# Layer 1 with tokens on the partitions: 512 moving columns, h turned by DMA, layer 2 four products later

## The chip, the cores and the metric

The kernel runs on one core of one Trainium2 chip. The metric is the device time in microseconds, the median of several runs. All of the work is in one launch; inputs and outputs are float32 in DRAM.

## The reference

Sliding-window attention with a linear bias is followed by a mixture of eight experts. After attention, x has 4608 tokens of 512 values. Cut to what matters:

```python
logits = x @ w_gate                      # 4608 x 8
P = np.exp(logits - logits.max())
for _ in range(8):                       # rows and columns in turn
    P /= P.sum(1, keepdims=True) + 1e-09
    P /= P.sum(0, keepdims=True) + 1e-09
    P *= N / E
out = np.zeros((N, D))
for e in range(8):
    h = np.maximum(x @ w1[e], 0.0)       # 512 -> 1024
    out += P[:, e:e + 1] * (h @ w2[e])   # 1024 -> 512
```

Every token goes through every expert; P only weights the results.

## The kernel before, in words

**Two stages.** To about 320 us the kernel computes attention, one batch after the other, and fills TensorE's gaps with both layers of experts 0 and 1 (`Filler`, `unit_atoms`, whose layer 2 is L159); their unweighted results go to DRAM (`ysp`), and x goes there too, by token (`xd`). Then P is balanced in eight rounds (`balance`). The second stage, from about 321 us to the end, does experts 2 to 7. It is the one that changes.

**The second stage** walks 108 units, a unit being 256 tokens and one expert: 18 groups of 256 tokens, experts 2 to 7 inside each. Matrices are cut in quarters, and each layer is done in Strassen's way with seven products instead of eight. Units 4 and 5 (experts 6 and 7 of the first group) do layer 1 plainly, since their weight sums are not yet made (`l1_bank`, L990), and the last unit does layer 2 plainly (`plain`, L1115).

**Layer 1 of a unit.** ScalarE scales the 256 tokens of x by that expert's P (`scale_x`, L923: P is not negative, so relu(P x w) is P relu(x w)), SP turns the result by two DMA transposes so that features are on the partitions (`turn_xs`, L935), and VectorE forms four sums (`sums_x`, L947). Seven parts follow (`part`, L1014), each of eight matmuls at L1020 with 128 weight columns stationary and 128 tokens moving. They add up in three PSUM banks A, B and C; between them ScalarE copies A to B (L1182), C to `s5` (L1186) and B to C (L1194), since sums are shared. h then leaves as four quarters (slots 0 to 3 of `hs`): slots 0 and 2 straight by relu, slots 3 and 1 by an add of `s5` on VectorE (L1203, L1209) and a relu in place (L1033). Features are on the partitions, which is what layer 2 needs of its stationary operand.

**Layer 2 of a unit.** `make_sums` (L1035) forms the sums of h's quarters on VectorE, and `product` (L1048) runs seven products of four matmuls with 256 moving columns (L1057). The products of the six experts of a group add up in four PSUM banks (`Ms`); at the group's end `gather` (L1082) adds them into `acc`, `begin` (L1069) brings in experts 0 and 1 from `ysp` (loaded by `load_y`), and `finish` (L1103) writes `acc` out.

**Order.** It is written out by hand in the loop at L1163. Each engine takes its instructions in the order of the program. TensorE alternates a part of unit n with a product of unit n-1. `scale_x` and `turn_xs` work two units ahead. `some` feeds VectorE sums of weights that later experts need, in the first eleven units. SP's queue carries the turns, the loads of x and y and the stores of the output; POOL's queue carries loads of weights, the last of them `load_w2` of expert 7 for the plain layer 2 of the last unit.

Of the kernel before, what the change touches and what calls it, by code (L numbers as in the profile page):

```python
# [14 lines left out]
def kernel(  # L15
# [20 lines left out]
    P = 128  # L36
# [68 lines left out]
    def unit_atoms(e, b0, nb, pool, tag, bufs, finish):  # L105
# [5 lines left out]
        halves = 2 if e == 0 and b0 < RI else 1  # L111
# [140 lines left out]
    if True:  # L252
# [649 lines left out]
        N = len(units)  # L902
        HF = Fd // 2
        h: dict = {}
        Ms: dict = {}
# [4 lines left out]
        xtok = [acc.rearrange("p m d -> p (m d)").bitcast(FP16)[:, HD * i : HD * i + HD] for i in range(2)]  # L910
        xs = [xset[i // 2][:, 4 + 2 * (i % 2) : 6 + 2 * (i % 2), :].rearrange("p q n -> p (q n)") for i in range(4)]

        def strassen(n):
            return n >= E - 2 or units[n][1] < E - 2

        def load_x(g):
            for m in range(2):
                nc.sync.dma_start(out=xtok[m], in_=xd[2 * g + m])

        load_x(groups[0])  # L920
        balance(7)

        def scale_x(n):  # L923
            if n >= N:
                return
            g, e = units[n]
            for m in range(2):
                blk = 2 * g + m
                nc.scalar.mul(out=xs[2 * (n % 2) + m], in_=xtok[m], mul=P_sb[:, blk, e : e + 1])  # L929
            if e == E - 1 and n + 1 < N:  # L930
                if g == groups[0]:
                    xtok[:] = [per.tile([P, HD], FP16, name=f"xtok_{i}", tag="yo", bufs=YO) for i in range(2)]
                load_x(units[n + 1][0])

        def turn_xs(n):  # L935
            if n >= N:
                return
            for m in range(2):
                nc.sync.dma_start(
                    out=xset[n % 2][:, 2 * m : 2 * m + 2, :].rearrange("p q (d t) -> p (q d) t", t=P),  # L940
                    in_=xs[2 * (n % 2) + m],
                    transpose=True,
                )
# [3 lines left out]
        def sums_x(n):  # L947
            if n >= N or not strassen(n):
                return
            x = xset[n % 2]  # L950
            nc.vector.tensor_tensor(out=x[:, T1 : T3 + 1], in0=x[:, B12 : B22 + 1], in1=x[:, B11 : B12 + 1 : 2], op=ALU.subtract)
            nc.vector.tensor_tensor(out=x[:, T2], in0=x[:, T3], in1=x[:, B11], op=ALU.add)
            nc.vector.tensor_tensor(out=x[:, T4], in0=x[:, B21], in1=x[:, T2], op=ALU.subtract)
# [33 lines left out]
        def new_h(n):  # L987
            h[n] = per.tile([P, 8, NF2, P], FP16, name=f"hs_{n}", tag="hT", bufs=2)

        def l1_bank(n, i):  # L990
            g, e = units[n]
            if i == 0:
                new_h(n)
            x = xset[n % 2][:, 0:4].rearrange("p q (d t) -> p (q d) t", t=P).rearrange("p (b d) t -> p d b t", b=2)
            ps = aps.tile([P, 2, HB], FP32, name=f"psh_{n}_{i}", tag="pmm", bufs=4)
            for f in range(2):
                ft = 2 * i + f
                for dt in range(NDT):
                    nc.tensor.matmul(  # L999
                        out=ps[:, f, :],  # L1000
                        lhsT=W1L[e][:, dt, P * ft : P * ft + P],
                        rhs=x[:, dt],
                        start=(f == 0 and dt == 0),
                        stop=(dt == NDT - 1),
                        skip_group_check=True,
                    )
            fh, j = 2 * (i // 2), 2 * (i % 2)
            nc.scalar.activation(
                out=h[n][:, fh : fh + 2, j : j + 2, :].rearrange("p t f k -> p f t k"),
                in_=ps.rearrange("p f (t k) -> p f t k", t=2),  # L1010
                func=AF.Relu,
            )

        def part(n, ps, w, x, start=False):  # L1014

            q = SL[units[n][1]][w]
            q = q if isinstance(q, list) else [q[:, k] for k in range(2)]
            for j in range(NF2):
                for k in range(2):
                    nc.tensor.matmul(  # L1020
                        out=ps[:, j, :],
                        lhsT=q[k][:, P * j : P * j + P],
                        rhs=xset[n % 2][:, x, P * k : P * k + P],
                        start=(start and j == 0 and k == 0),
                        stop=(k == 1),
                        skip_group_check=True,
                    )

        def bank(n, name):
            return aps.tile([P, NF2, P], FP32, name=f"ps{name}_{n}", tag="pmm", bufs=4)  # L1030

        def relu(n, slot, src):
            nc.scalar.activation(out=h[n][:, slot], in_=src, func=AF.Relu)  # L1033

        def make_sums(n):  # L1035
            t = h[n]
            nc.vector.tensor_tensor(out=t[:, 4:6], in0=t[:, 0:2], in1=t[:, 2:4], op=ALU.add)  # L1037
            nc.vector.tensor_tensor(out=t[:, 6:8], in0=t[:, 1:4:2], in1=t[:, 0:3:2], op=ALU.subtract)
            nc.vector.tensor_tensor(out=t[:, 1], in0=t[:, 0], in1=t[:, 3], op=ALU.add)

        LEFT = {3: 0, 4: 3, 5: 4, 2: 5, 6: 6, 7: 7, 1: 1}
        RIGHT = {1: "f1", 2: "q11", 3: "f3", 4: "f4", 5: "q22", 6: "f6", 7: "f7"}
        BANK = {3: (0, 0), 4: (0, 1), 5: (1, 0), 2: (1, 1), 6: (2, 0), 7: (2, 1), 1: (3, 0)}

        def ends(n):
            return n >= 0 and units[n][1] == (E - 2 if units[n][0] == groups[-1] else E - 1)

        def product(n, *which):  # L1048
            if n < 0:
                return  # L1050
            g, e = units[n]
            for m in which:
                bk, half = BANK[m]
                if bk not in Ms:
                    Ms[bk] = mps.tile([P, 2, 2 * P], FP32, name=f"psM_{bk}")
                for f in range(NF2):
                    nc.tensor.matmul(  # L1057
                        out=Ms[bk][:, half, :],
                        lhsT=h[n][:, LEFT[m], f, :],
                        rhs=W2L[e][RIGHT[m]][:, f, :],  # L1060
                        start=(e == 2 and f == 0 and half == 0),
                        stop=(ends(n) and f == NF2 - 1 and (half == 1 or m == 1)),
                        skip_group_check=True,
                    )

        def load_y(g, e):
            nc.sync.dma_start(out=y, in_=ysp[e, 2 * g : 2 * g + 2].rearrange("m p d -> p m d"))
# [14 lines left out]
        def gather(g, *which):  # L1082
            q4 = acc.rearrange("p m (c n) -> p (m c) n", c=2)
            for m in which:
                bk, half = BANK[m]
                ps = Ms[bk][:, half, :]
                for lo, step, op in {
# [53 lines left out]
        while filler.l1 or filler.todo or len(filler.l2) > 3:  # L1141
# [3 lines left out]
            if pieces == 2:  # L1145
                scale_x(1)
                turn_xs(1)
# [138 lines left out]
```

## Time and profile before

| | |
|---|---|
| median of three runs | 1003.1 us (1002.57 to 1004.06) |
| the profiled execution | 1001.61 us |
| its span, first to last instruction | 999.8 us |
| TensorE, VectorE, ScalarE busy in 360 to 960 us | 100%, about 79%, about 83% |
| DMA engines' mean busy share, 500 to 900 us | 0.35 to 0.41 |
| HBM read and written | 78.30 MB, 23.59 MB |

In the profile PE is TensorE's matmuls, PEld its weight loads, DVE VectorE, ACT ScalarE, POOL GpSimd and SP the engine that issues most DMAs. A row of groups gives line, engine and operation, output and inputs, shape and count, then busy time and the mean of one, then the idle time before it and who ended it. Matmuls are pipelined, so the duration of one (219 ns for 128 columns) says less than the distance between two starts. A timeline row gives start, length, engine, line and count. Of a DMA the profile gives the time its issue takes on the queue and the time to its landing.

### The profile page before, as it was taken

How to read it: one execution, taken by the hardware profiler on the slowest of the kernel's cores; microseconds unless marked ns; L12 is line 12 of the kernel's file. 1: busy time of each engine (PE TensorE's matmuls, PEld its weight loads, DVE VectorE, ACT ScalarE, POOL GpSimd, SP SyncE). 2: the span in 40 equal slices, each digit the busy share in tenths (PEclk: the TensorE clock that was granted, in tenths of full speed). 3: DMA queues.
4: the chain of work that ended last, by engine and by line, in shares of the span. 5: the costliest groups of instructions: out<-in, count | busy, mean ns of one | idle time of the engine just before them, and what ended most of it. 6: DMA issues, size and time to landing. Idle time of an engine off the chain costs nothing.

```text
span 999.8 us, 28277 instructions
## 1 busy us (share of the span) xinstructions
PE 988.3 (99%) x11731; PEld 816.0 (82%) x11731; DVE 762.0 (76%) x1593; ACT 718.0 (72%) x1216; POOL 110.0 (11%) x202
## 2 busy tenths in 40 slices
PE   7999999999999999999999999999999999999998
PEld 5645665566545899999999999999999999999997
DVE  5737677665688989887887787787787787787787
ACT  7655545554435768888888888888888888888885
POOL 3314444354110000000000000000000000000000
PEclk9999999999999999999999999999999999999999
DMA  9998999989997324333333433333433433333371
GB/s 250 212 271 218 187 233 230 234 170 183 222 201 152 81 54 97 82 61 94 86 56 95 86 76 75 88 73 75 96 76 65 99 78 65 96 76 66 96 116 49
DMA packets 264978, 123.08 MB, mean 123 GB/s; under 512 B 204433, under 2 KB 255633, under 8 KB 264849
## 3 DMA queue, kind: packets, MB, share of 16 engines
q1 hardware_dynamic: 249152, 100.65, 45.4%
q0 software_dynamic: 15264, 20.46, 11.5%
q8 instruction: 92, 1.51, 0.6%
q14 instruction: 38, 0.30, 0.1%
q10 hardware_dynamic: 432, 0.16, 0.1%
HBM read 78.30 MB, written 23.59 MB: 102 GB/s over the span
## 4 chain that ended last, share of the span: by engine, by line
PE 91%; DVE 5%; ACT 2%; DMA 1%; issue 1%; DVEq 0%; ACTq 0%
PE psM L1057 31%; PE psB L1020 14%; PE psy L159 11%; PE psA L1020 9%; PE psC L1020 9%; PE psh L137 9%; PE psh L118 3%; PE psS L457 1%; PE psN L491 1%; DVE pt L468 1%; DMA k<-in_k_dram 1%; ACT pt L463 1%; PE psh L999 1%; DMA xset<-xs 1%; DVE xsb L502 1%
## 5 line engine op out<-in xcount | busy, mean ns | idle before, releaser
L1057 PEld LDWEIGHTS <-hs 128*128 128x128 f16 x2996 | 271.0, 98 | 22.4 <-DVE hs L1037 0.4
L1057 PE MATMUL psM<-w2l,hs 128*128 128x256 f16 x1440 | 186.6, 273 | 0.2 <-DVE hs L1037 0.2
L1020 PEld LDWEIGHTS <-w1l 128*128 128x128 f16 x2848 | 181.4, 98 | 4.8 <-issue 0.4
L1033 ACT ACTIVATE hs<-hs 128x512 f16<-128x512 f16 x212 | 130.4, 629 | 36.2 <-DVE hs L1203 26.6
L1203 DVE TENSOR_TENSOR hs<-psB,s5y 128x512 f16<-128x512 f32 x106 | 73.3, 692 | 97.9 <-ACT xs L929 92.2
L1020 PEld LDWEIGHTS <-s 128*128 128x128 f16 x2136 | 141.6, 98 | 6.7 <-issue 0.2
L929 ACT ACTIVATE xs<-xtok,L_sb 128x512 f16<-128x512 f16 x204 | 135.8, 720 | 2.1 <-DMA xset<-xs 2.1
L159 PE MATMUL psy<-w2t,hT 128*128 128x512 f16 x576 | 135.3, 379 | 0.0
L1057 PE MATMUL psM<-more,hs 128*128 128x256 f16 x864 | 129.5, 273 | 0.0
L1020 PE MATMUL psB<-xset,s 128*128 128x128 f16 x1424 | 108.5, 219 | 0.1
L1020 PE MATMUL psA<-xset,w1l 128*128 128x128 f16 x1424 | 108.5, 219 | 0.0
L149 ACT ACTIVATE hT<-psh 128x512 f16<-128x512 f32 (+1 forms) x104 | 60.1, 581 | 63.5 <-PE psh L137 63.4
L159 PEld LDWEIGHTS <-hT 128*128 128x128 f16 x576 | 54.0, 98 | 58.2 <-issue 1.1
L463 ACT ACTIVATE pt<-psS 128x1024 f16<-128x1024 f32 x64 | 64.6, 1022 | 50.4 <-PE psS L457 49.9
L137 PE MATMUL psh<-xT,w1t 128*128 128x512 f16 (+1 forms) x448 | 99.0, 364 | 0.0
L1037 DVE TENSOR_TENSOR hs<-hs 128x1024 f16<-128x1024 f16 x107 | 73.9, 691 | 20.6 <-ACT hs L1033 18.6
L1194 ACT COPY psC<-psB 128x512 f32<-128x512 f32 x106 | 60.4, 570 | 38.6 <-PE psB L1020 38.6
L579 DVE CAST yo<-psy 128x512 f16<-128x512 f32 x65 | 44.6, 690 | 50.8 <-PE psy L159 50.1
L1186 ACT COPY s5y<-psC 128x512 f32<-128x512 f32 x106 | 62.2, 587 | 22.4 <-PE psC L1020 22.4
L615 POOL DMA_DIRECT2D w2t<-in_moe_w_dram x2 | 1.8, 882 | 669.0 <-PE psA L1020 661.0
L468 DVE TENSOR_TENSOR pt<-pt,mask 128x1024 f16<-128x1024 f16 x64 | 53.6, 837 | 28.3 <-ACT pt L463 28.1
L1101 DVE TENSOR_TENSOR acc<-acc,psM 128x256 f32<-128x256 f32 (+1 forms) x162 | 73.9, 503 | 0.3
(131 smaller groups left out, 1548.8 us busy)
## 6 DMA issues: line engine op xcount, KB each, us to landing
s5y<-ysp SPq DMA_DIRECT2D x36, 256.0 KB, 3.0
ysp<-yo SPq DMA_DIRECT2D x65, 128.0 KB, 4.4
v<-in_v_dram SPq DMA_DIRECT2D x32, 256.0 KB, 4.6
out_dram<-acc SPq DMA_DIRECT2D x31, 256.0 KB, 2.5
q<-in_q_dram SPq DMA_DIRECT2D x5, 1024.0 KB, 6.4
k<-in_k_dram SPq DMA_DIRECT2D x5, 1024.0 KB, 9.2
xtok<-xd SPq DMA_DIRECT2D x34, 128.0 KB, 2.3
w2t<-in_moe_w_dram POOLq DMA_DIRECT2D x4, 1024.0 KB, 12.3
```

The costliest lines, as they stand in the source:

```text
L137: nc.tensor.matmul(out=ps[:, 0:nt], lhsT=w1ts[e][:, dt, P * ft : P * ft + P], rhs=xT[:, at : at + nb, dt, :], start=(dt == 0), stop=(dt == ...
L159: nc.tensor.matmul(out=ps, lhsT=st["hT"][:, ft, P * ms : P * ms + P], rhs=w2ts[e][:, ft, :], start=(ft == 0), stop=(ft == NFT - 1),)
L463: nc.scalar.activation(out=pt, in_=ps.rearrange("p a y n -> p (a y) n"), func=AF.Exp, scale=scale)
L468: nc.vector.tensor_tensor(out=pt, in0=pt, in1=mask_of[kb][:, 4 * u : 4 * u + 4, :], op=ALU.mult)
L929: nc.scalar.mul(out=xs[2 * (n % 2) + m], in_=xtok[m], mul=P_sb[:, blk, e : e + 1])
L1020: nc.tensor.matmul(out=ps[:, j, :], lhsT=q[k][:, P * j : P * j + P], rhs=xset[n % 2][:, x, P * k : P * k + P], start=(start and j == 0 and ...
L1033: nc.scalar.activation(out=h[n][:, slot], in_=src, func=AF.Relu)
L1037: nc.vector.tensor_tensor(out=t[:, 4:6], in0=t[:, 0:2], in1=t[:, 2:4], op=ALU.add)
L1057: nc.tensor.matmul(out=Ms[bk][:, half, :], lhsT=h[n][:, LEFT[m], f, :], rhs=W2L[e][RIGHT[m]][:, f, :], start=(e == 2 and f == 0 and half = ...
L1101: nc.vector.tensor_tensor(out=a, in0=a, in1=p2, op=op)
L1186: nc.scalar.copy(out=s5, in_=pc)
L1203: nc.vector.tensor_tensor(out=h[n][:, 3], in0=pb, in1=s5, op=ALU.add)
```

## The change

Layer 1 of experts 2 to 7 is turned round. x is no longer scaled: it is loaded and turned once per group and its four sums are made once per group (`turn_x2`, `sums_x(gi)`). In `part` x is the stationary operand (128 tokens) and the weights move, 512 columns at a time, so a part is two matmuls; h comes out with tokens on the partitions. There each token's P is one value per partition, and the relu takes it as its scale. A quarter of h lies in `hr` (four buffers, one per slot) and SP turns it by a DMA transpose into `hs` (`turn_h`), four turns per unit. The sums of h are five single adds (`sum_h`). Layer 2 runs later: in a step, TensorE does products 6, 1, 5 and 7 of unit n-2 and then 3, 4 and 2 of unit n-1; to that end the products' sums rotate through five PSUM banks (`sum_of`), the fifth taken from the pool of layer 1. The order of a step is a string of tokens, one for each expert, with special ones for units 0, 1, 4, 5 and the last. Outputs, y and x are issued on POOL's queue (`nc.gpsimd`). The last leftover unit of expert 1 has its layer 2 cut in halves, six of which (before: three whole ones) are done in units 0 and 1.

The diff, cut to its core:

```diff
-        halves = 2 if e == 0 and b0 < RI else 1
+        halves = 2 if (e == 0 and b0 < RI) or (e == 1 and b0 == NBLK - 4) else 1
...
-        def scale_x(n):
...
-        def turn_xs(n):
...
+        def turn_x2(gi, m):
+            nc.sync.dma_start(
+                out=xset[gi % 2][:, 2 * m : 2 * m + 2, :].rearrange("p q (d t) -> p (q d) t", t=P),
+                in_=xst[m],
+                transpose=True,
+            )
...
+        def part(n, name, w, x, start=False):
...
-            for j in range(NF2):
-                for k in range(2):
-                    nc.tensor.matmul(
-                        out=ps[:, j, :],
-                        lhsT=q[k][:, P * j : P * j + P],
-                        rhs=xset[n % 2][:, x, P * k : P * k + P],
...
+            for k in range(2):
+                nc.tensor.matmul(
+                    out=psum(name),
+                    lhsT=xset[n // NE % 2][:, x, P * k : P * k + P],
+                    rhs=q[k],
...
         def relu(n, slot, src):
-            nc.scalar.activation(out=h[n][:, slot], in_=src, func=AF.Relu)
+            g, e = units[n]
+            blk = 2 * g + slot % 2
+            nc.scalar.activation(out=hr[slot], in_=src, func=AF.Relu, scale=P_sb[:, blk, e : e + 1])
+
+        def turn_h(n, slot):
...
+            nc.sync.dma_start(out=hs[n % 2][:, slot], in_=hr[slot], transpose=True)
+
+        def add_h(n, slot, name):
+            nc.vector.tensor_tensor(out=hr[slot], in0=psum(name), in1=s5, op=ALU.add)
+            relu(n, slot, hr[slot])
+            turn_h(n, slot)
+
+        def sum_h(n, to):
...
+                5: (1, 3, ALU.add),
+                6: (1, 0, ALU.subtract),
+                1: (0, 3, ALU.add),
+                4: (0, 2, ALU.add),
+                7: (3, 2, ALU.subtract),
...
+        ORDER = (3, 4, 2, 6, 1, 5, 7)
...
+        def sum_of(g, m):
+            bk = (4 * groups.index(g) + BANK[m][0]) % 5
...
-            nc.sync.dma_start(out=y, in_=ysp[e, 2 * g : 2 * g + 2].rearrange("m p d -> p m d"))
+            nc.gpsimd.dma_start(out=y, in_=ysp[e, 2 * g : 2 * g + 2].rearrange("m p d -> p m d"))
...
-        while filler.l1 or filler.todo or len(filler.l2) > 3:
+        while filler.l1 or filler.todo or len(filler.l2) > 6:
...
+        plans = (
+            "a11 t5 X s1 X s2 t6 a12 X X s3 s4 T0 p+ X X c+ a22 t4 t1 t7 X",
+            "a11 s1 X g2 X s2 g4 X g3 a12 s3 T0 s4 X g5 p+ c+ t5 X a22 X t7 X t6 t4 t1 Y0 XL0",
+            "a11 g6 g7 X s1 s2 a12 g1 FIN X X T0 s3 p+ s4 X t5 c+ t4 X a22 XT0 X X t6 t7 t1 XL1",
+            "a11 X s1 X t5 s2 X X a12 T0 s3 X p+ s4 X X c+ t6 t1 B0 t7 a22 t4 XT1 Y1",
+            "a11 s1 X X s2 a12 X T0 s3 p+ s4 X c+ t5 X a22 X t6 X SX t7 t4 t1",
+            "a11 s1 X s2 a12 X s3 X T0 p+ s4 X c+ t5 X a22 t6 t1 t4 X X B1 t7",
+        )
+        first = {
+            0: "a11 s1 W W F s2 a12 F T0 W W s3 p+ s4 c+ F W W a22 F",
+            1: "a11 s1 F s2 a12 F T0 s3 p+ s4 c+ t5 t6 X t1 X t4 a22 X t7 Y0",
...
+            N - 1: "a11 s1 X B1 s2 a12 X t5 s3 X T0 p+ s4 X c+ X t6 a22 X t1 t4 g3 X t7 X g4 X g2 X g6 X g1 g5 g7",
+        }
+        sums_at = {1: 3, 2: 3, 3: 3, 4: 2, 5: 3, 6: 3, 8: 2, 9: 3, 10: 3}
...
+            if n == N - NE + 1:
                 load_w2(E - 1)
-        gather(units[N - 2][0], *late)
-        plain(N - 1, 0)
-        plain(N - 1, 1, 0, HB)
-        plain(N - 1, 1, HB, HD)
+        plain(1, "A", 0, HD)
+        plain(0, "C", 0, HB)
+        plain(0, "B", HB, HD)
```

How to read a plan: a11, s1, s2, a12, s3, s4 and a22 are the parts, with the copies, relus and (for slot 2) the turn that belong to them; p+ and c+ are the adds, relus and turns of slots 3 and 1; T0 turns slot 0; X is the next product; t5, t6, t1, t4, t7 are the sums of the h of unit n-1; g are gathers, B0 and B1 `begin`, FIN `finish`, Y and XL loads of y and x, XT turns of x, SX the sums of x; W is a weight sum and F a leftover half of expert 1's layer 2. `sums_at` adds weight sums right behind the first token.

## The prediction

> **What bounds the kernel now.** I read the page first: its busy rows, its 40 slices and its groups.
>
> ```profile
> span 999.8 us, 28277 instructions
> PE 988.3 (99%) x11731; PEld 816.0 (82%) x11731; DVE 762.0 (76%) x1593; ACT 718.0 (72%) x1216; POOL 110.0 (11%) x202
> ...
> PE   7999999999999999999999999999999999999998
> ...
> PEclk9999999999999999999999999999999999999999
> DMA  9998999989997324333333433333433433333371
> ...
> q8 instruction: 92, 1.51, 0.6%
> ...
> L1057 PE MATMUL psM<-w2l,hs 128*128 128x256 f16 x1440 | 186.6, 273 | 0.2 <-DVE hs L1037 0.2
> ...
> L1203 DVE TENSOR_TENSOR hs<-psB,s5y 128x512 f16<-128x512 f32 x106 | 73.3, 692 | 97.9 <-ACT xs L929 92.2
> L929 ACT ACTIVATE xs<-xtok,L_sb 128x512 f16<-128x512 f16 x204 | 135.8, 720 | 2.1 <-DMA xset<-xs 2.1
> L159 PE MATMUL psy<-w2t,hT 128*128 128x512 f16 x576 | 135.3, 379 | 0.0
> ```
>
> TensorE is busy in 99% of the span, at full granted clock, with almost no wait. The others have room: DMA sits near 3 tenths in the last 27 slices, the stage that changes (321 us to the end). ScalarE's scaling of x (136 us) only makes VectorE wait. So this stage goes as fast as TensorE streams, and what counts is how far apart its matmuls start. The timeline of one unit shows it:
>
> ```profile
> 702.28 0.61 PE L1020 MATMUL psC<-xset,s 128*128 128x128 f16 x8
> 702.73 0.60 PE L1057 MATMUL psM<-more,hs 128*128 128x256 f16 x4
> 703.16 0.61 PE L1020 MATMUL psB<-xset,s 128*128 128x128 f16 x8
> ```
>
> Eight small matmuls take 0.45 us from start to start, four of layer 2 0.44. Over 370 to 955 us the spacings are 55.8 ns (128 columns) and 109.2 ns (256). A unit has 56 and 28: 3.127 + 3.057 = 6.184 us, and the chain of work repeats every 18.55 us for three units. The 512-column matmuls of L159, each with weights of its own, stand 215.9 ns apart.
>
> **The sum, term by term.**
>
> *TensorE.* A part becomes two 512-column matmuls: 14 x 215.9 = 3.022 us instead of 3.127. The products stay. A unit costs 6.079 us, 0.105 less; for 106 units -11.1 us. The two plain units go from 32 x 109.2 to 16 x 215.9 ns, -0.08. Together **-11.2 us**, and that is the floor: the small parts already streamed near the column rate. The halved weight loads (98 ns each) lie beside matmuls before and after.
>
> *ScalarE, VectorE, POOL.* Two scalings a unit go (1.33 us); the relus take a scale, as L929 has one (720 against 629 ns, but 0.61 us apart). x is turned and summed once per group: five sixths of 1.0 us of VectorE a unit go. The five h sums are now single 128x512 adds (425 ns, 0.34 apart), 1.75 us a unit for 1.8. Both engines have more room than before, so I cost them at nothing where their order fits. I walked it with rows: ScalarE starts 0.42 us after the last 512-column matmul starts (L149 after L137), so copy A to B ends 0.63 + 0.57 = 1.20 us after part a11 begins; s2, which needs it, comes three blocks later at 1.30. The copy that s3 waits for has the same 0.1 us. If this cover went, each late tenth would cost about 10 us over 106 units. Outputs, y and x move from SP to POOL's queue, where nothing runs after 313 us and an issue takes 0.88 us; their users come 3 us or more later. The one that SP waits for, the second half of the next x, is there 2.4 us into expert 6's step, and SP reaches it at 3.5. At nothing.
>
> *Layer 2 waits for h by DMA.* This is the new wait. Behind SP's turn of slot 1 hang the sum t5 (VectorE) and product 2 (TensorE, where everything queues). These rows price a turn:
>
> ```profile
> L939 SPq DMA_TRANSPOSE xset<-xs x212: 1188/1192/2493, 325.6 to 979.2; - x106
> ...
> DMA to landing us min/median/max: 2.4/2.5/6.8
> ```
>
> SP issues one in 1.19 us, back to back every 1.31 us, and it lands after 2.5. There were 2 a unit; now 4, and 2 more per group: 26 x 1.31 = 34.1 us of a group's 36.5. And 26 of 193 turns between 362 and 955 us took 0.83 us longer; each of them had a 16 KB packet of q8 (instructions) beside it. Those packets come every 9.4 us; TensorE's instructions halve, so about every 18, and SP's denser turns meet two a group: 1.7 us. SP is then busy 35.8 of 36.5 us.
>
> The walk, for expert 7's step and the next, in us from the step's start, blocks of 0.43: s3 starts at 2.60 and can be read at 3.23; add p+ ends at 3.9, relu 3 at 4.6; s4 starts at 3.47, add c+ ends at 4.8, relu 1 at 5.5. SP comes from the two steps of five turns (experts 4 and 5; 6.6 us of SP in a unit of 6.1) with a backlog: T0 goes at 4.0 though relu 0 was done at 3.2, slot 3 at 5.35, slot 1 at 6.67; it lands at 9.2, 3.1 into expert 2's step. There t5 and t6 (0.35 each) stand ahead of p+ on VectorE, and a22, due at 5.2, waits for p+: t5 must start by 3.8. That leaves 0.7 us; in the other steps t5 comes later in the order and has 1.3 to 2 us. One slow turn (0.83) in the half of the group before it overruns the 0.7 by 0.15. I take 0.17 us a group, over 17 or 18 groups **+3 us**; the ends are 0 (spare elsewhere) and +8 (rival C). It cannot gain.
>
> *The start.* Step 0 puts two weight sums (0.61 apart) and a cast (0.69) in VectorE's queue after a leftover half product of expert 1 (0.87 us of TensorE) and ahead of p+: the cast can start at 3.66 us, so p+ ends at 6.2, and a22, due at 5.2, waits 1.0. In step 1 t5 ends 0.3 after product 2 is due. In step 8 two weight sums push gather 7 to 2.5 us, and product 1, which takes over its bank, is due at 2.2: 0.4. The page's stretch 328 to 336 us shows 0.3 idle that goes. **+1.4 us**; ends 0 (VectorE ahead) and +3 (each twice as bad).
>
> *The last weight load.* load_w2 of expert 7 fires once. Before, POOL issued it at 961.77 us, and the chain shows what the next turn paid:
>
> ```profile
> 965.28 6.77 DMA xset<-xs
> 972.08 1.33 ACT xs L929 x2
> ```
>
> 6.77 us for a turn against 2.5, 4.3 more. There it was x, needed a unit later, and TensorE lost 0.1 us. Now it is h: unit 103's slot 1 is issued at about 6.4 us of its step, as the load begins, lands 6.8 to 8.5 us later, and product 2 is due at 11.7: t5 ends near 15, 3.3 late, and sums queued behind cost 0.4 more; group 16's outputs now stand in POOL's queue behind the load. I take **+4 us**; ends 0.1 (hidden as before) and 7.
>
> What the Trainium skill says of it ("DMA: Bandwidth & Descriptors", Queues, rings and completion order): a DMA engine takes turns between the queues that have work, packet by packet. By that rule a turn beside the load would take perhaps twice its time, and the sum would be about 3 us lower (rival B). The 6.77 us disagrees for the load's first part.
>
> *The tail* (last parts, 24 matmuls of layer 2, output) keeps its work; four products are only later, and the halves swap so that slot 2 is read last. In the last step relu 2 ends at 6.3 us, SP turns it at 7.6, it lands at 10.1 and is needed at 10.2. Before, a22 waited for L1203 near 991.7 for some 0.3 us. Even; 0.5 us either way.
>
> Sum: -11.2 + 3 + 1.4 + 4 = **-2.8 us**. 999.8 becomes 997.0. The profiled execution took 1001.61, 1.8 above its span, and the median, 1003.1, is 1.5 above that; so 1000.3.
>
> **Rivals.**
>
> *A. Everything is hidden.* t5's spare time is enough in all steps and the start and the load cost 0 to 3 us: -11.2 + 1.5 = -9.7, 993.4 (991.9 to 995). For it: TensorE's 100% and the freed engines. Against: SP at 35.8 of 36.5 us and the 6.77 us.
>
> *B. The load shares the engines with the turns.* Between 969 and 972 us, load and turns do run together (DMA share 1.32). If so from the start, a turn of 0.65 us of data lands about 0.7 us late, the load term is 0.7 instead of 4, and the time 997.0. The rule of the Trainium skill cited above would have it so. The 6.77 us speaks against it.
>
> *C. SP's queue becomes the clock: slower.* If turns with their slow ones average not 1.31 + 1.7/26 = 1.375 us but 1.42, as before (1.31 + 26 x 0.83/193), a group needs 36.9 us of SP, 0.45 above TensorE's 36.5; in 18 groups +8 instead of +3: 1005.3. With SP also idle 0.15 us a unit, waiting in order for relu 0, another 16: 1021. It gives back the whole gain once a group of turns takes 36.8 us, 1.415 a turn. For it: measured mean and room of 2%. Against: fewer instruction packets, and plain DMAs leave SP.
>
> *D. The wide parts don't stream faster.* If two take what eight small ones took (0.447 us), the gain is 0 and the rest +8.4: 1011.5. L159 has just this shape at 215.9 ns, so little.
>
> **Chances.** The forecast's case (late waits of 3 to 13 us, 995 to 1005) 0.42, A 0.18, B 0.12, C 0.20, D 0.08. About 0.2%, 2 us, is what a measurement can tell from no change: faster is under 1001.1, slower over 1005.1. Faster: 0.30 of the forecast's, all of A, 0.11 of B: 0.59. Same: 0.11 + 0.01 + 0.05 of C: 0.17. Slower: 0.01 + 0.15 of C + D: 0.24. The range 993 to 1010 leaves out the lower part of A (0.07), the far part of C (0.06) and of D (0.06). Faster cases alone run 992 to 1001.
>
> **What would show it.** L1020's successor at 216 ns spacing and a unit of 6.08 us in the chain: TensorE's term. TensorE's waits naming t5 or the sums (DVE on hs), clustered in the steps of experts 7 and 2: the h term; none there is A; in every unit, with SP solid in its timeline, is C. One gap of 3 to 4 us after the w2t load: that term; no gap is B. Gaps ahead of a22 near 326 us: the start. I am wrong if the copies on ScalarE come after s2 or s3 (0.1 us of cover), which would show as short waits for ACT in each unit.

## The result, and the profile after

The changed kernel takes 1065.7 us (median of 5 runs, 1057.2 to 1075.4) against 1002.6 for the kernel before on the same chip: a ratio of 1.060, with a 95% interval of 1.0555 to 1.0642. The run of 1075.4 fell in a slow state and is left out of the ratio; without it the median is 1063.9, and the differences below start from that. It is 6% slower, far above the range of the prediction.

The page of the changed kernel: first the span, the first busy row, two of the rows of 40 slices, and three DMA queues (packets, MB, share of 16 engines' time).

```profile
span 1064.0 us, 19659 instructions
...
PE 998.4 (94%) x7247; PEld 623.9 (59%) x7247; DVE 693.7 (65%) x1543; ACT 627.3 (59%) x1000; POOL 177.5 (17%) x310
...
PEclk9999999999999999999999999999999999999989
DMA  9999799989994665655656566564665655665684
...
q1 hardware_dynamic: 366592, 110.90, 52.5%
q0 software_dynamic: 22560, 43.27, 19.5%
q8 instruction: 56, 0.92, 0.4%
```

TensorE executes 7,247 matmuls instead of 11,731 and is idle for 65.6 us of the span (1064.0 less 998.4); before, it was idle for 11.5. The DMA engines are busy 5 to 6 tenths of the last stage instead of 3 to 4. The instruction packets fell from 92 to 56, as foreseen.

Was it the matmuls? The timeline of one unit, in the columns of the one shown for before (start, length):

```profile
699.80 0.59 PE L979 MATMUL psB<-s,xset 128*128 128x512 f16 x2
700.23 0.59 PE L979 MATMUL psC<-w1l,xset 128*128 128x512 f16 x2
700.66 0.60 PE L1059 MATMUL psM<-w2l,hs 128*128 128x256 f16 x4
701.10 0.60 PE L1059 MATMUL psM<-more,hs 128*128 128x256 f16 x4
```

A part of two wide matmuls takes 0.43 us from start to start where eight small ones took 0.45. So the stream is as fast as forecast wherever it runs. What TensorE waited for, from 340 us on (total us, times, longest; before, this list held one wait of 0.2 us):

```profile
PE psB L979 <- DVE hr L1016: 32.3, 26, 6.4
PE psM L1059 <- DVE hs L1031: 17.6, 23, 1.6
PE psB L979 <- ACT psB L1169: 2.3, 7, 0.9
```

L1016 is the add of h (`add_h`: p+ and c+), L1031 the sums of the turned h (`sum_h`: t5 and its like). Both kinds stand on VectorE. In the same list for all engines, VectorE's own waits have one cause in common:

```profile
DVE hs L1031 <- DMA hs<-hr: 101.0, 60, 4.7
...
DVE hr L1016 <- DMA hs<-hr: 29.9, 20, 8.4
```

The sums wait for a turn to land. The adds wait for a turn too, but for another reason: they write the single tile hr of a slot, which the turn of the unit before must have read. A group of six units, worked out from the starts of its part a11, now takes 40.43 us in the mean (one takes 47.0, the median is 40.0); six times 6.079 is 36.47.

### The profile page after: what moved, and what is told of

Same layout as the page of the kernel before. It is cut to its first block, busy times and chain, and to the rows that moved or that the text cites. A ratio compares the mean times of both kernels' runs of the same rounds, so it can differ in the third digit from the quotient of the medians.

```text
span 1064.0 us, 19659 instructions
## 1 busy us (share of the span) xinstructions
PE 998.4 (94%) x7247; PEld 623.9 (59%) x7247; DVE 693.7 (65%) x1543; ACT 627.3 (59%) x1000; POOL 177.5 (17%) x310
## 4 chain that ended last, share of the span: by engine, by line
PE 66%; DMA 20%; DVE 7%; issue 3%; ACT 3%; SPq 1%; POOL 0%; DVEq 0%; ACTq 0%; POOLq 0%
PE psM L1059 20%; DMA hs<-hr 16%; PE psy L159 11%; PE psB L979 9%; PE psh L137 8%; PE psC L979 6%; PE psA L979 6%; PE psh L118 3%; DVE hr L1016 3%; DVE hs L1031 2%; ACT hr L1008 1%; PE psN L491 1%; DMA q<-in_q_dram 1%; PE psS L457 1%; DVE acc L1101 1%
## 5 line engine op out<-in xcount | busy, mean ns | idle before, releaser
L1059 PEld LDWEIGHTS <-hs 128*128 128x128 f16 x2996 | 289.5, 98 | 169.8 <-DVE hs L1031 35.5
L1031 DVE TENSOR_TENSOR hs<-hs 128x512 f16<-128x512 f16 x535 | 201.0, 418 | 103.7 <-DMA hs<-hr 101.0
L1008 ACT ACTIVATE hr<-hr,L_sb 128x512 f16<-128x512 f16 x212 | 148.2, 719 | 169.6 <-DVE hr L1016 167.4
L1059 PE MATMUL psM<-w2l,hs 128*128 128x256 f16 x1440 | 211.8, 274 | 15.4 <-DVE hs L1031 14.7
L979 PEld LDWEIGHTS <-xset 128*128 128x128 f16 x1484 | 145.2, 98 | 120.2 <-issue 44.2
L1016 DVE TENSOR_TENSOR hr<-psB,s5y 128x512 f16<-128x512 f32 x106 | 73.0, 688 | 106.0 <-PE psB L979 86.1
L979 PE MATMUL psB<-s,xset 128*128 128x512 f16 x356 | 105.7, 378 | 1.5 <-ACT psB L1169 1.4
L979 PE MATMUL psA<-w1l,xset 128*128 128x512 f16 x356 | 106.8, 382 | 0.4 <-ACT hr L1008 0.4
L1101 DVE TENSOR_TENSOR acc<-acc,psM 128x256 f32<-128x256 f32 (+1 forms) x162 | 74.4, 504 | 30.8 <-PE psM L1059 29.9
L1008 ACT ACTIVATE hr<-psA,L_sb 128x512 f16<-128x512 f32 x110 | 75.9, 690 | 19.9 <-PE psA L979 16.4
L979 PE MATMUL psB<-w1l,xset 128*128 128x512 f16 x178 | 53.7, 383 | 33.3 <-DVE hr L1016 33.3
L1016 DVE TENSOR_TENSOR hr<-psC,s5y 128x512 f16<-128x512 f32 x106 | 72.6, 685 | 16.3 <-DMA hs<-hr 12.2
L1008 ACT ACTIVATE hr<-psB,L_sb 128x512 f16<-128x512 f32 x108 | 72.5, 671 | 17.6 <-DMA hs<-hr 14.7
```

The costliest lines, as they stand in the source:

```text
L979: nc.tensor.matmul(out=psum(name), lhsT=xset[n // NE % 2][:, x, P * k : P * k + P], rhs=q[k], start=(start and k == 0), stop=(k == 1), ski ...
L1008: nc.scalar.activation(out=hr[slot], in_=src, func=AF.Relu, scale=P_sb[:, blk, e : e + 1])
L1016: nc.vector.tensor_tensor(out=hr[slot], in0=psum(name), in1=s5, op=ALU.add)
L1031: nc.vector.tensor_tensor(out=t[:, to], in0=t[:, x], in1=t[:, y], op=op)
L1059: nc.tensor.matmul(out=ps, lhsT=hs[n % 2][:, LEFT[m], f, :], rhs=W2L[e][RIGHT[m]][:, f, :], start=(e == 2 and f == 0 and half == 0), stop= ...
L1101: nc.vector.tensor_tensor(out=a, in0=a, in1=p2, op=op)
```

## The experiments

All times are medians beside runs of the kernel before on the same chip; these lay at 1001.9 to 1003.2. "Group" is the mean time of six units. My main theory after reading the trace had three parts: (1) in expert 3's step gather 5 waits for product 7 and holds up p+; (2) h's turns come late; (3) the last weight load holds turns back. The rivals are with each run.

| run | what differs from the changed kernel | us | ratio (95%) | group |
|---|---|---|---|---|
| changed kernel | | 1063.9 | 1.060 | 40.43 |
| e1 | gather 5 behind a22 | 1037.0 | 1.033 [1.031, 1.036] | 38.43 |
| e2 | no turns of h from unit 2 | 1015.2 | 1.012 [1.010, 1.014] | 37.74 |
| e3 | e1 and e2 | 993.6 | 0.990 [0.989, 0.992] | 36.49 |
| e4 | no last weight load | 1049.3 | 1.047 [1.044, 1.049] | |
| e5 | e1, no turn of slot 2 | 1011.0 | 1.009 [1.007, 1.010] | 37.0 |
| e6 | e1, nearly no transfers from POOL | 1021.6 | 1.019 [1.017, 1.021] | 37.6 |
| e9 | e1, last load in eight pieces | 1029.1 | 1.028 [1.025, 1.030] | 38.5 |
| e10 | e9, slots 3 and 1 turned together | 1029.9 | 1.029 [1.025, 1.033] | 37.5 |
| e11 | e10, order mended, more y buffers | 1038.0 | 1.037 [1.034, 1.040] | 39.07 |
| e12 | e11, two tiles for the joint turn | 1023.6 | 1.022 [1.017, 1.028] | 37.65 |
| e13 | lag of five, slots 1 and 2 together | 1001.6 | 0.999 [0.997, 1.001] | 36.67 |
| e14 | e13 with four turns a unit | 1021.2 | 1.018 [1.016, 1.020] | 38.01 |
| e15 | e13, y buffers given back | 997.7 | 0.995 [0.993, 0.997] | 36.68 |

### Gather 5, the turns, and both (e1, e2, e3)

e1 edits one plan, that of expert 3's step:

```diff
-"... s4 X g5 p+ c+ t5 X a22 X t7 X t6 t4 t1 Y0 XL0",
+"... s4 X p+ c+ t5 X a22 X t6 g5 X t7 t4 t1 Y0 XL0",
```

> One token moved: in the step of expert 3, gather 5 goes from before the add p+ to behind a22 (and t6 ahead of it). Theory: gather 5 waits for product 7, which shares its PSUM bank, so p+ and with it a22 come 1.17 us late in each of 18 groups; without that some 18 us less than the change's 1065.7, so 1045 to 1050. Rival 1: those gaps only give the turns of h time to catch up, and the waits for h take them back: 1060 to 1066. Rival 2: the order of VectorE has nothing to do with it: unchanged, a22 still 1.17 us late.

e2 leaves the turns of h out:

```diff
 def turn_h(n, slot):
+    if n >= 2:
+        return
```

> The turns of h are left out from unit 2 on (layer 2 goes on with the h of units 0 and 1; 424 of 432 turns gone, all else as in the change). Theory: of 73 us of gaps on TensorE some 20 are gather 5's, some 5 the start's, and the rest, with the gap at the last load of weights, hangs on turns that land late: 1065.7 - 45 = about 1020. Rival: the order on VectorE and ScalarE is what is late, turned h or not: above 1045.

e3 has both edits.

> Both edits at once: gather 5 later, and no turns of h from unit 2 on (layer 2 goes on with old h). Theory: nothing but the start is left on TensorE's path, a unit takes 6.08 us and the time is 993 to 998, which is the prediction's term of -11.2 us by itself. Rival: wide matmuls or clock cost something of their own: a unit over 6.15 us and above 1003.

The timeline of the changed kernel shows the first part in one step of expert 3 (in brackets: idle time before, and what ended it):

```profile
533.43 0.60 PE L1059 MATMUL psM<-w2t,hs 128*128 128x256 f16 x4
...
534.07 0.75 DVE L1101 TENSOR_TENSOR acc<-acc,psM 128x256 f32<-128x256 f32 x2 [1.25 <-PE psM L1059]
534.74 0.68 DVE L1016 TENSOR_TENSOR hr<-psB,s5y 128x512 f16<-128x512 f32 x1
...
535.48 0.59 PE L979 MATMUL psB<-w1l,xset 128*128 128x512 f16 x2 [1.01 <-DVE hr L1016]
```

Product 7 is the first line. Gather 5 (L1101) idles 1.25 us until it is done, although product 5, which it reads, ended long before: both are halves of one psM tile, a bank. Behind gather 5 on VectorE stands p+, and behind p+ on TensorE a22, which starts 1.0 us late. The list of TensorE's waits in e2, where no turn is left, holds this and nearly nothing else, once in each of the 17 groups that have the step:

```profile
PE psB L979 <- DVE hr L1018: 17.1, 17, 1.0
```

From start to start it is 1.17 us, so 20 us in 17 groups; e2 to e3 measures 21.7. Part 1 is shown. With the turns in, moving gather 5 brought 26.9 (1063.9 to 1037.0), more than the 16 to 21 that e1's theory gave it. That a late p+ also makes its unit's turns late would explain the rest; no run shows it by itself. e2 came out 5 us below its theory, e3 within its own.

e3, the same program with neither, is the stream alone:

```profile
span 991.6 us, 18527 instructions
...
PE 978.3 (99%) x7247; PEld 626.4 (63%) x7247; DVE 686.6 (69%) x1543; ACT 624.5 (63%) x1000; POOL 177.5 (18%) x310
```

Its group of 36.49 us is 6.08 a unit. So all that keeps the changed kernel from 993.6 is gather 5 and the turns (with what holds those up): 70 us, of which e1 to e3 gives the turns 43.

### The last load (e4, e9)

e4 leaves the load of expert 7's w2 ahead of the plain last unit out; e9 is e1 with the load cut in eight pieces, two behind each of the units 103 to 106:

```diff
-if n == N - NE + 1:
-    load_w2(E - 1)
+if N - NE + 1 <= n < N - 1:
+    load_w2(E - 1, 2 * (n - N + NE - 1), 8)
+    load_w2(E - 1, 2 * (n - N + NE - 1) + 1, 8)
```

> The last load of weights (load_w2 of expert 7, 1 MB) is left out, so the last unit's layer 2 uses what the buffer holds. Theory: the turns of units 103 and 104 no longer land after 7 to 11 us, the two gaps of together 6.8 us ahead of a22 in unit 104 go, and with them the stretch at a lower granted clock behind them: 8 to 10 us less, 1056 to 1058. Rival (the prediction's term): 4 us, 1062. Rival 2: the gap is taken back by other late turns: 1065.

> On top of gather 5 later (1037.0 us): the last load of weights in eight pieces of 128 KB, two behind each of units 103 to 106, instead of 1 MB at once. Leaving it out took 16 us from the change. Theory: turns then wait for one piece (about 1 us) and not for 7 us of load: 8 to 14 us less, 1023 to 1029. Rival: POOL runs the pieces back to back and nothing changes: 1035 to 1038.

e4 gained 14.5 us, more than the 8 to 10 of its theory, and e9 7.9 over e1; the prediction had 4. Not all of e4's gain is the load's. The load is issued behind unit 103, and from the start of unit 102 to the end the changed kernel's trace takes 56.0 us and e4's 47.7: 8.2 us, as the theory has it. The other 11 us between the two traces lie ahead of unit 102, where the programs are the same, 4.7 of them in one group (units 60 to 65, 47.0 us against 42.3); their cause is not shown. Nor do the traces show e9's 7.9: unit 104 takes 6.13 us there instead of e1's 12.98, but a turn of unit 106 landed after 7.30 us, and from the start of unit 107 to the end it took 20.0 us instead of 15.2. That run is the slowest of e9's four (1033.7), and e1's the fastest of its four (1034.3).

The chain of waits of the changed kernel (start, us, what) shows the load's effect:

```profile
1019.99 0.62 ACT hr L1008
...
1020.74 11.15 DMA hs<-hr
...
1032.02 0.70 DVE hr L1016
...
1032.76 1.01 PE psB L979 x2
```

Relu 3 ends, its turn is issued at 1020.74 and lands 11.15 us later; only then may the next unit's p+ overwrite slot 3's hr, and a22 waits for that. Unit 104 took 13.88 us. The DMA queues in the window 1021 to 1024 us, of which this is the whole list that moved anything:

```profile
q0 software_dynamic: 419, 0.43, 104.0%
```

For these 3 us POOL's queue (the load, and an output beside it) has all 16 engines, and SP's has no packet although turns are issued. The page "DMA: Bandwidth & Descriptors" of the Trainium skill (Queues, rings and completion order) has an engine take turns, by packet, between the queues that have work; by that I estimate half of the engines for the turn. The measurement shows none for that time, and it decides; whether SP's queue had packets ready then, or got them late, the trace does not tell. Later the two queues do share: q1 has 21% in the next 3 us, then 50 and 74%.

After the gap some matmuls ran at a lower clock. The table by stretch (PE, PEld, DVE, ACT and POOL busy, granted clock, DMA share, GB/s):

```profile
720.00:740.00 20.00, 16.38 (x103) 10.13 (x101) 11.53 (x26) 9.65 (x16) 1.27 (x2) 0.91 0.46 86
...
1020.00:1040.00 20.00, 13.56 (x77) 8.29 (x77) 7.06 (x17) 7.97 (x13) 1.12 (x2) 0.83 0.85 125
```

0.83 and 0.91 stand in the two stretches with TensorE's longest waits, 6.4 and 2.6 us; 760 to 780 us, with no wait over 1.3, shows 0.91 as well. At 730 us, behind the wait of 2.6, a part then takes 0.85 us from start to start instead of 0.43. Without the load (e4) the clock is 1.00 from 980 to 1040 us; with the load in pieces (e9), where the longest gap there is 2.8 us, still 0.91 from 1000 to 1020. "TensorE: Matmul & The Clock Gate" of the Trainium skill (Part 1: The HAM clock gate) has the array fall to half its clock after an idle window of about 3.4 us and return after as much work. The wait of 6.4 us agrees with that; the waits of 2.8, 2.6 and 1.3 are shorter than the page's figure, and the clock fell there too. The prediction had no price for it.

### How many turns, and who shares the engines (e5, e6)

```diff
 # e5, in part_of
-    turn_h(n, 2)
+    if n < 2:
+        turn_h(n, 2)
 # e6, in step: y, x and outputs only for the first groups
-if gi > 0:
+if gi == 1 or gi == len(groups) - 1:
```

> On top of gather 5 later (1037.0 us): the turn of slot 2 is left out from unit 2 on (106 turns fewer, product sums with old slot 2), so that SP issues 20 turns a group instead of 26. Theory: what is left in the steady groups, 1.9 us each, is SP's queue, a backlog of turns 1.31 us apart; with 20 turns it empties in each step and the gaps before product 2 in expert 6's step (0.93 us in each group) go: 1005 to 1012, the last load's gap being all that stays. Rival: it is transfers on POOL's queue that hold up single turns, however many there are: above 1025.

> On top of gather 5 later (1037.0 us): the loads of y and x and the stores of the output on POOL's queue are left out for nearly all groups (results go unwritten), all turns stay. Theory (SP's queue): turns are as dense, but those that landed after 3 to 4.5 us land after 2.5, which is part of the lateness: 1022 to 1030, with product 2 of expert 6's step still late. Rival (POOL's transfers are the cause): 1005 to 1012. Second rival: no part in it, 1037.

Leaving out one turn of four brought 26.0 us over e1, leaving out POOL's transfers 15.4. e5 fell within its theory's range and e6 just below its own, far from its rival's. Both matter, the turns more; but e5 also lets nothing wait for slot 2 and spares the engines its bytes, so by itself it doesn't price SP's queue. The rows of the turns in the changed kernel:

```profile
L1013 SPq DMA_TRANSPOSE hs<-hr x432: 1188/1208/3088, 324.7 to 1056.2; - x144
...
DMA to landing us min/median/max: 2.4/2.5/11.2
```

The median of 2.5 us hides the tail: of the 466 turns (x's 34 among them), 144 landed after more than 3.25 us (worked out from their records; the mean is 3.04). Of the kernel before's 212 turns, 56 did. A landing was thus not much slower than before; it was late only now, when VectorE had a sum or an add waiting for it. In e6 the mean is 2.72. SP's issues that follow each other directly stand 1.397 us apart in the mean, in stretches of up to 18: 26 at that distance are 36.3 us of the 36.5 that TensorE needs. Over all turns between 370 and 945 us SP's issues, with the 0.1 us behind each, came to 35.5 us of a group's 40.4, close to the prediction's 35.8; for the other 5.0 SP stood idle between turns.

### Turning two slots at once, at the old lag (e10, e11, e12)

One DMA may turn 1024 columns. e10 puts slots 3 and 1 into one tile and turns them once, behind c+:

```diff
+if slot in (1, 3):
+    nc.sync.dma_start(out=hs[n % 2][:, 1:3].rearrange("p s f t -> p (s f) t"),
+                      in_=h13.rearrange("p s f -> p (s f)"), transpose=True)
+    return
```

> Gather 5 later, the last load in pieces, and slots 3 and 1 turned by one DMA of 1024 columns instead of two of 512 (the attention stage's turns of 2048 columns take SP 1.85 us at least, against 4 x 1.19, so about 1.4 instead of 2.5 us; a buffer less in two places makes room). SP then needs some 30 us of a group's 36.5. Theory (SP's queue): h comes in time and the time is 995 to 1003, faster than both kernels. Rival: a turn that waits for both slots lands too late for product 2, and the merged transfer holds up others: 1015 to 1030.

The turn cost SP 1.23 us, as the expectation's theory needs, and the group fell by 1.0 us to 37.5. But the tile's 2 KB came from the first stage's y buffers (`yo`, seven to five), and unit 1 started at 342.8 us instead of 328.7; the gain went there. The time lies in the rival's range for that reason.

e11 gives the first stage two buffers elsewhere, turns x a step earlier, moves some sums, and paces the load's pieces through units 104 to 106:

> What is built in: gather 5 behind a22 in expert 3's step; slots 3 and 1 of h turned by one 1024-column DMA (four turns of SP's queue per unit become three); the last weight load in eight pieces, paced through units 104 to 106; the turns of x a step earlier; t5 earlier in the steps of experts 2 and 6, the shared sum ahead of SX in expert 7's step; two weight sums of steps 0 and 8 moved behind the adds; two of every seven y buffers of the first stage in another pool, so that the merged turn's tile does not shorten that stage's buffering as it did in the run before. Theory (what was lost is gather 5's bank, h that SP's queue turns too late, and the load, and nothing else): the group falls to 36.5 to 36.8 us, the first stage ends at about 328.7 us as in the kernel before, no unit of the last four takes over 7 us, and the time is 994 to 1000, below the kernel before. Rival (the turns land late because x, y and output transfers on the DMA engines share them, not because of their number): merging does not bring them in time, the group stays at 37.3 to 37.6 us and the time is 1005 to 1015. Should the first stage still start unit 1 more than 3 us late, the buffers were the cause there and the group alone decides.

It missed on both: unit 1 started at 329.9, so the buffers were the cause there, but the group rose to 39.07. In the list of waits VectorE's add of slot 3 waited for the joint turn 81.7 us: slot 3's half of the tile stays taken until slot 1's turn has landed. e12 makes it two tiles, one for even and one for odd units:

> The run before with a second tile for the merged turn, so that the add and relu of slot 3 no longer wait until the turn of the unit before has read the one tile. Room for it comes from the constants' tiles, from s5 in fp16, and from y buffers of the first stage kept elsewhere. Theory (in the run before, VectorE's add of slot 3 waited 81.7 us in 31 places for the merged turn to have read its tile, and the relus queued behind it on ScalarE delayed the copies and so s2; that chain made most of its 39.07 us per group): with two tiles the group falls to 36.5 to 37.2 us and the time to 996 to 1008. Rival (the merged turn itself lands too late, after 3.2 us in the median and 4.5 to 7.6 in one of six): the waits move to the products that use slots 1 and 3, the group stays above 37.8 us, and the time is 1015 to 1030.

The group fell to 37.65, above what the theory gave it, with 23.9 us of gaps left after unit 1, 14.7 of them ahead of product 4, which reads slot 3: that now lands with slot 1. The theory was half right, and the rival too: joining slots 3 and 1 makes slot 3 late. (The first stage lost 9 us again.)

### More lag, and four turns against three (e13, e14, e15)

e13 lets layer 2 lag by five products, with one order in all steps, all sums behind the adds, gathers behind both products of their bank, and slots 1 and 2, ready within a microsecond of each other, turned together. The plan of most steps becomes

```diff
-"a11 s1 X s2 a12 X s3 X T0 p+ s4 X c+ t5 X a22 t6 t1 t4 X X B1 t7",
+"a11 s1 X s2 a12 X s3 X T0 p+ s4 X c+ X a22 t5 t6 t1 t4 t7 X X B1",
```

so that the sums are needed only in the next step. e14 is e13 with a turn for each of slots 1 and 2.

> Layer 2 lags by five products instead of four, with one order of the seven parts and seven products in every step but one; all sums of h stand behind both adds, so that each has an eighth to half of a step of spare time more; gathers of a group's outputs stand behind the products they share a bank with; slots 1 and 2 (ready within 1 us of each other) are turned by one 1024-column DMA and slots 0 and 3 by one each, three turns of SP a unit; the last load in eight paced pieces; first stage as in the run with one tile for the merged turn (about 1 us late there). Theory (the changed kernel lost its time because layer 2's order left the turns less time than they take on the chip, and because gather 5 waited for its bank's other half): with more time the group is 36.5 to 36.8 us and the whole 994 to 1000, below the kernel before. Rival (the turns are too slow at any such lag, since they share the DMA engines with POOL's transfers): the group stays above 37.3 us and the time is above 1008.

> The same, but slots 1 and 2 turned by a DMA each, four turns of SP a unit and 26 a group with x, as in the changed kernel. It tells the lag from the number of turns. If SP's number of turns is the clock (26 of 1.31 us and slow ones of 0.83 us more are 35.8 us if two of them are slow and 36.8 or more if four), the group is 36.8 to 37.6 us and the time 1001 to 1014; if it was only the time that each turn had, the group is 36.5 to 36.7 us and the time within 2 us of the merged one.

e13 has 4.0 us of gaps after unit 1; e14 has 27.8, and is 20 us slower. e13's group is what its theory said, its time is above it because of the start; e14 came out above its ranges for a queue that is the clock, in group and time, and far above those for time alone. The two programs differ in the joint turn alone: three issues a unit instead of four, and with it the moment of slot 1's turn and a little of the engines' time (SP's queue q1 has 53.3% of 1000.5 us in e13, 55.5% of 1019.6 in e14, 6% more). So it is the number of turns that costs, and SP's queue is the likely place; that the 6% has no part in it is not shown. The lag alone, with the order that came with it, brought some 8 us (e9, with four turns at the old lag, is at 1029.1). e14's waits of TensorE, and of the others behind them:

```profile
PE psB L986 <- ACT psB L1181: 14.8, 17, 1.7
PE psC L986 <- DVE h L1023: 4.1, 8, 0.8
```

```profile
DVE hr L1023 <- DMA hs<-hr: 21.0, 6, 4.4
DVE h L1023 <- DMA hs<-h: 18.1, 13, 2.6
ACT h L1015 <- DMA hs<-h: 12.8, 18, 1.8
```

No sum is in the first list any more. The turns now show through their source tiles: relu 2 waits on ScalarE until the last turn has read its tile, the copy A to B queues behind it, and s2 waits for the copy. Directly following issues stand 1.411 us apart, in stretches of up to 25; 26 at that distance would be 36.7 us, over TensorE's 36.5. Over all turns between 370 and 945 us, though, SP was busy 35.8 us of a group's 38.0 and idle 2.2, in about four places: it need not be full to be late. SP's timelines, e14 first (start, time of that many issues):

```profile
699.21 2.52 SPq L1020 DMA_TRANSPOSE hs<-h  x2
701.84 2.53 SPq L1020 DMA_TRANSPOSE hs<-hr  x2
704.47 3.44 SPq L1020 DMA_TRANSPOSE hs<-h  x2
708.01 2.53 SPq L1020 DMA_TRANSPOSE hs<-hr  x2
```

```profile
700.25 1.19 SPq L1030 DMA_TRANSPOSE hs<-hr  x1
701.64 1.23 SPq L1024 DMA_TRANSPOSE hs<-h  x1
702.92 1.27 SPq L925 DMA_TRANSPOSE xset<-xst  x1
704.33 3.70 SPq L1030 DMA_TRANSPOSE hs<-hr  x2
708.11 1.26 SPq L1024 DMA_TRANSPOSE hs<-h  x1
710.41 2.77 SPq L1030 DMA_TRANSPOSE hs<-hr  x2
```

In e14 each issue begins 0.1 us after the last has ended; in the second, of e15, SP is idle for 1.0 us before the last line: it has caught up and waits for a relu. e13's unit 1 started at 334.3 us, 5.6 later than in the changed kernel, for want of y buffers: one cast waited 6.6 us for the store of the buffer it was to fill. e15 lends the joint turn's tile to that stage until the last one begins:

```diff
+h12 = lp.tile([P, 2, HD], FP16, name="h12")
+elif kept_y[0] % 7 in (2, 5) and not held:
+    yo = closed[0][:, int(kept_y[0] % 7 == 5)]
```

> The run with five products of lag and three turns a unit, with the merged turn's tile lent to the first stage as two more y buffers until the last stage begins. Theory (only those buffers delayed the first stage): unit 1 starts at 329 us or earlier instead of 334, the group stays at 36.5 to 36.7 us, and the time is 994 to 998, faster than the kernel before by 0.4 to 0.8%. Rival (the first stage's stores are late for another reason, such as SP's order): unit 1 still starts at 330 to 334 us and the time is 998 to 1002.

Unit 1 started at 327.8 us and the whole took 997.7 us, 0.5% below the kernel before (ratio 0.9931 to 0.9969). Its page and all of TensorE's waits from 340 us on:

```profile
span 994.7 us, 19606 instructions
...
PE 979.6 (98%) x7247; PEld 625.8 (63%) x7247; DVE 703.2 (71%) x1543; ACT 624.5 (63%) x1000; POOL 183.6 (18%) x325
```

```profile
PE psB L989 <- DVE hr L1033: 1.4, 1, 1.4
PE psB L989 <- ACT psB L1191: 0.9, 1, 0.9
PE psC L989 <- DVE h L1033: 0.5, 1, 0.5
```

53 us of waits (the list of the changed kernel) became 2.8, with the same matmuls.

## Why the prediction was wrong

**TensorE's term, -11.2 us, was right.** e3, which runs the stream without turns and without gather 5's wait, is 9.6 us below the kernel before (0.9904 of 1003.2), with the start's waits, below, still in it. Its parts stand 0.43 us apart, its unit takes 6.08. Rival D is out.

**"I cost them at nothing where their order fits. I walked it with rows" failed.** The recorded walk has no wait for gather 5: it took it to run once product 5 was done. It had to wait for product 7 in the other half of the same bank: 1.17 us in each of 17 groups, 20 us, nearly twice TensorE's term. I had used the rule of the shared bank for step 8, where a product takes over a gather's bank, and not the other way round, for a gather that waits for the product beside it. The wait can be found from the plan and BANK alone: in expert 3's step g5 stands right behind the fourth X, which is product 7, and ahead of p+.

**"I take 0.17 us a group" failed, at 3.94 us measured a group** (40.43 less 36.49), 1.17 of it gather 5. The rest, 2.8 us a group or 1.9 with gather 5 moved (e1), is turns that come late. The place was wrong as well. Summed by step from unit 6 on, TensorE waited only 1.6 us in expert 7's steps and 6.7 in expert 2's, but 12.2 in expert 6's, right behind the two steps with five turns, where the walk had 1.3 to 2 us to spare; with gather 5 moved (e1) these are 14.6 of 27.6 us. (Expert 3's have 17.8, of which 16.1 are waits for p+, behind gather 5.) Three things in the step were wrong. First, every turn was taken to land after 2.5 us and to be late only by its issue; a quarter of the turns of before already landed after more than 3.25 us, but a row of minimum, median and maximum does not show it. Second, spare time was reckoned for one slow turn in a step, while SP, busy for 35.8 of 36.5 us by my own sum, can hardly make up lost time: delays are handed on, as stretches of up to 18 turns back to back suggest. The sum itself was right (35.5 and 35.8 measured, in the changed kernel and e14); that such a load still leaves the turns in time was not. Third, the walk had turns waited for only by the sums that read hs. It left out that a turn holds its source: hr has one tile a slot, and p+, c+ or the relu of the next unit waits for it (29.9 us on VectorE in the changed kernel).

**Rival C was nearest to the mechanism, at a chance of 0.20.** It put the turn's mean against 1.415 us; 1.397 was measured in the changed kernel and 1.411 in e14, so by C's own threshold SP would hardly have been the clock. Four turns against three cost 20 us all the same (e14 against e13): a queue that needs some 36 of every 36.5 us need not pass the limit to make its consumers wait. e14, with gather 5, the lag and the load mended, comes closest to C alone, at 1021.2. That C's far end was 1021 is partly luck: C had 36.9 us of turns a group and 0.9 of idle time, e14 has 35.8 and 2.2.

**The last load, +4 us, was about 8** (8.2 behind unit 102 in the traces of the changed kernel and e4; the medians give 14.5 for leaving it out and, with gather 5 moved, 7.9 for cutting it up). That the load holds SP's turns up was right, and rival B (the engines are shared) is out for its first microseconds. But the price came from 6.77 us; here a turn took 11.15, the hold went through the source tile to p+ rather than through t5, and TensorE then ran at half its granted clock for 6.8 us (0.50 from 1030.9 to 1037.7 us).

**The start, +1.4 us,** came out at 3.3 in e3, just above its far end of 3. Steps 0 and 1 wait 1.15 and 0.3 us, as named; step 8 waits 1.0 instead of 0.4; 0.56 each ahead of units 5 and 6 was not foreseen; and the 0.3 of before is gone. **The tail** showed nothing that these runs can tell from none.

What stays open: how the 43 us of the turns (e1 to e3) divide between landings and SP's rate. e5, e6, e9 and e13 (against e14) each take one share out, and their shares (26, 15, 8 and 20 us) overlap and sum to more. Nor was it tried to give slots 0 to 3 two source tiles each at the old lag.

## What to carry to other kernels

Count a DMA queue that feeds the engine in front as a resource with its own utilisation, and leave it room: SP was 98% full by the prediction's own sum, a slow issue could hardly be made up, and at a lag of five products six issues less in 26 were worth 20 us. When a gather or an add is placed by hand, list what shares its bank or its source tile, in both directions, before the durations. If work is to hide behind a DMA, plan for its late landings, not its median, and check by a run with the DMA left out what the rest would take: it gave the floor, 993.6 us, in one run.

## What the runs showed of the hardware

A turn of 1024 columns costs SP hardly more than one of 512 (rows of e15: duration of an issue in ns, minimum, median, maximum), and lands after 3.2 us in the median instead of 2.5:

```profile
L1030 SPq DMA_TRANSPOSE hs<-hr x216: 1188/1191/2460, 325.0 to 984.5; - x108
```

```profile
L1024 SPq DMA_TRANSPOSE hs<-h x108: 1231/1232/1499, 329.6 to 985.8; - x108
```

While a 1 MB load and an output stood on POOL's queue, SP's queue moved no packet for 3 us, and a turn landed after 11.15 us; without the load (e4) none took over 6.0. And TensorE's granted clock fell to 0.83 and 0.91 in the mean of the 20 us around waits of 6.4 and 2.6 us, and to 0.91 around one of 1.3.
